# Decay attention into a mixture of experts on one core: the reciprocals of the row sums are spread by ScalarE, and the order of all steps is laid out anew

## The chip, the core and the metric

The kernel runs on one core of a Trainium2 chip. Its engines work side by side, each through its own instructions in order: TensorE (PE: matmuls; its weight loads are PEld), VectorE (DVE), ScalarE (ACT), GpSimd (POOL) and SyncE (SP), which here issues the DMA transfers. Engines wait for each other on semaphores. The metric is the device time of one execution in microseconds (us). For the kernel before it is 650.12 us, the median of three runs (650.10, 650.12, 650.39).

## What is computed

```python
# decay attention, B=8, H=8, S=576, D=64
scores = (q @ k.T) / sqrt(D) + cum[i] - cum[j]      # cum = cumsum(log f); causal
attn   = exp(scores - rowmax) / (rowsum + 1e-9)
x      = (attn @ v)                                  # laid out as [B, S, 512]
# mixture of E=4 experts, the best K=2 for each row
w      = softmax over the two best logits of x @ w_gate
for e in range(E):                                   # each expert is a causal attention on x
    y_e  = softmax(causal((x @ wq[e]) @ (x @ wk[e]).T / sqrt(64))) @ (x @ wv[e]) @ wo[e]
    out += (e is chosen) * w_e * y_e
```

## The kernel before

**Units.** The work is cut into 48 units of two heads or two experts: `a{b}_{p}` is head pair p (0 to 3) of batch b, `m{b}_{p}` expert pair p (0 or 1). Each unit goes through the same generators, and a name ends in its unit (`ka_a1_1` is tile ka of unit a1_1):

- `prep_attn` makes the operands of the scores. All products are made in two parts, a rounded value and its rest; the rests of a head pair are two subtractions at L406 (64x1152 each, on VectorE for nearly all pairs), into `ka`, which the scores read. For the experts `moe_front` (gates at L504 to L532) and `prep_moe` (matmuls `pp` at L551) do this.
- `max_pass` finds a maximum for each row: matmuls into `m` (L625), masked maxima on VectorE at L631, L647, L680 and L687 into `mxs`, a transposition of `mxs` on TensorE (`mp`, L692), and from there ScalarE (`ms`, L695) and a DMA into the operand `kq`.
- `scores` makes the products s0 to s3 (L726 reads `ka`, L727 reads `kq`), ScalarE takes the exponentials into `P` and `pl` (L744 to L784), GpSimd cuts them at the diagonal (L713, L747, L786) and adds them to the row sums `R` (L792 to L798).
- `attend` multiplies by the values (L817) and ScalarE brings the result to `ot` (L841, L843).
- `row_sums` does two units at once, so there are 24 of them: 16 of heads, 8 of experts. Matmuls with a column of ones make `sm`; VectorE transposes it into `zt` (L870), adds 1e-9 (L873), takes the reciprocal `rc` of 18 columns (L875; experts: times the gate, L878), spreads each of these 18 numbers over 32 equal columns of `zt` (L881, 128x576, called the fill below), and transposes that into `rr` (L884). A DMA spreads `rr` to `bt`, with which `apply_rows` multiplies `ot` (L902). The tile of a row_sums is named by the first unit of the two: `zt_a0_2` holds the sums of a0_2 and a0_3.
- `project_out` multiplies by wo (`po`, L952), and the result leaves by DMA.

**Order.** Each generator stops at every `yield`. A table of two-digit numbers, ORDER, says which generator goes on next; another one, SLOTS, says which of a tile's buffers each use takes. At the end each engine's instructions are tied to the order in which they were written, so nothing overtakes on an engine. The two tables lay down the whole order of the kernel.

The loop that plays ORDER, and the tie:

```python
for x, y in zip(digits[::2], digits[1::2]):
    i = DIGITS.index(x) * len(DIGITS) + DIGITS.index(y)
    if i not in started:
        started[i] = iter(tasks[i]())
    next(started[i], None)
```

Of the kernel before, what the change touches and what calls it, by code (L numbers as in the profile page):

```python
# [32 lines left out]
040j0c0h0h0h0h0h0c0e0e0e0e0e030e08080e0e0e0e0e0e080808080808080e0808080e030e0o0e0h08080e080e04030j0j0j080e080808
080808080808080j0j0j0j0j0j0j08080o0t030o0o0f0f0j0j0j0j0j0j0j0j0j0j0j0j0j0j0o080A090j030f0j0h090v0o0t0j0q0f080f0f
0f0f0f0f0f0f090f0f0o080f0f0f0q0q0q0j0f0q0f0f0f0q0q0q0j0q0q0q0f0f0f0p0f0t0t0t0f4w4w4w080q0q0q0q0q0q0q030q0q0q0q0q
0q0q0i0A080f080q0f0t0k0k0k0k0k0k0k0k0k0k0k0k0k0f0k0o0a0q0q0q0k0k0k0k0a0k0k0k0k0k0k0a0a0v0v0v0v0a0a0v0v0v0v0v0k0F
0v0g0k0a0v0v0v0v0v0A0A0A0F0g0g0f0f0k0k0f0v0v0v0v0v0u0C0k0v0a0t0f0l0q0C0C0v0C0C0r0r4A0v0v0l040C0t0C0C0k0k0k0C0C0r
# [1022 lines left out]
```

## Time and profile before

| | us |
|---|---|
| median of three runs | 650.12 |
| the profiled execution | 650.38 |
| its span in the trace | 648.6 |
| TensorE busy | 629.9 (97%) |
| VectorE busy | 571.6 (88%) |
| GpSimd busy | 479.0 (74%) |
| ScalarE busy | 470.1 (72%) |
| mean granted TensorE clock | 0.996 of full speed |

The profile is of one execution. Its span runs from the first to the last instruction; 1.8 us of the execution lie around it. A row of a timeline gives the start of an instruction, its duration, the engine, the line, what it writes and reads, and in square brackets how long the engine stood idle ahead of it and who released it. Instructions overlap a little at their ends, so a start minus the start before is often the better price.

### The profile page before, as it was taken

What the parts mean: (1) busy time and instruction counts of PE and PEld (TensorE: products, weight loads), DVE (VectorE), ACT (ScalarE), POOL (GpSimd) and SP (SyncE); (2) the same over time, 40 slices, a digit from 0 to 9 for tenths busy, and PEclk for the clock granted to TensorE, in tenths of its full rate; (3) what the DMA queues carried; (4) which work ended last, traced back from release to release, by engine and by line L of the source; (5) the groups of instructions that cost most, each with busy time, mean ns of one, the idle gap of its engine ahead of it and who ended that gap; (6) DMA issues with size and microseconds to landing.
All of it is one profiled execution on the core that took longest, in us unless ns stands there. A gap on an engine that the chain in (4) does not pass through costs nothing.

```text
span 648.6 us, 15367 instructions
## 1 busy us (share of the span) xinstructions
PE 629.9 (97%) x5303; PEld 539.0 (83%) x5303; DVE 571.6 (88%) x1565; ACT 470.1 (72%) x1033; POOL 479.0 (74%) x759
## 2 busy tenths in 40 slices
PE   8898998999999999999999999999999999999997
PEld 6675898887978889889797898878988788979976
DVE  6899998999999989988989989999898999986762
ACT  7896785786769757797497875788768886556634
POOL 9999695878888776669578966967778758833850
PEclk9999998999999999999999999999999999999999
DMA  6556324443534454550643531753524632523125
GB/s 211 159 161 171 98 74 113 132 120 116 126 95 116 126 162 111 127 133 22 169 108 83 163 102 57 187 145 114 150 75 113 190 72 44 146 60 72 54 70 199
DMA packets 33532, 76.91 MB, mean 119 GB/s; under 512 B 4395, under 2 KB 4875, under 8 KB 33455
## 3 DMA queue, kind: packets, MB, share of 16 engines
q1 hardware_dynamic: 33455, 75.94, 43.4%
q8 instruction: 42, 0.69, 0.4%
q14 instruction: 35, 0.29, 0.1%
HBM read 32.86 MB, written 10.35 MB: 67 GB/s over the span
## 4 chain that ended last, share of the span: by engine, by line
PE 85%; DVE 9%; issue 2%; POOL 2%; ACT 1%; DMA 0%; SPq 0%; POOLq 0%; DVEq 0%; ACTq 0%
PE pp_m L551 15%; PE ob_a L817 9%; PE po L952 7%; PE pv L446 7%; PE s_a L726 7%; PE m_a L625 7%; PE s_a L727 6%; PE ob_m L817 4%; PE m_m L625 4%; PE s_m L726 4%; PE s_m L727 4%; DVE ka_a L406 3%; PE oa_a L817 3%; PE sm_a L855 2%; PE oa_m L817 2%
## 5 line engine op out<-in xcount | busy, mean ns | idle before, releaser
L726 PE MATMUL s_a<-ka_a 128*128 128x320 f32 (+4 forms) x384 | 105.0, 299 | 3.3 <-DVE mx_m L680 1.7
L727 PE MATMUL s_a<-kq 128*128 128x320 f32 (+4 forms) x384 | 103.6, 297 | 1.2 <-DMA kq<-ms_a 1.1
L631 DVE CUSTOM_DVE_ANT_0 junk_a<-m_a,mask 128x192 bf16<-128x192 f32 (+2 forms) x186 | 86.5, 484 | 7.7 <-PE m_a L625 4.1
L625 PE MATMUL m_a<-kq 128*128 128x448 f32 (+2 forms) x372 | 77.5, 302 | 1.7 <-DVE mxs_a L631 1.2
L713 POOL TENSOR_SCALAR_AFFINE_SELECT P_a<-P_a 128x128 f32<-128x128 f32 x128 | 53.1, 425 | 34.0 <-ACT P_a L762 17.6
L726 PEld LDWEIGHTS s_a<-ka_a 128*128 128x128 f32 (+1 forms) x384 | 70.1, 183 | 6.1 <-issue 4.1
L559 ACT ACTIVATE kq<-pp_m 64x288 fp32r<-64x288 f32 x128 | 51.8, 405 | 31.7 <-PE pp_m L551 29.8
L792 POOL TENSOR_TENSOR R_a<-P_a 128x448 f32<-128x448 f32 x64 | 73.5, 1149 | 0.0
L727 PEld LDWEIGHTS s_a<-kq 128*128 128x128 f32 (+1 forms) x384 | 69.6, 183 | 2.6 <-DMA kq<-ms_a 1.6
L564 DVE TENSOR_TENSOR ka_m<-pp_m,kq 64x288 fp32r<-64x288 f32 x128 | 58.3, 455 | 12.9 <-ACT kq L559 10.6
L817 PE MATMUL ob_a<-P_a,va 128*64 128x320 f32 (+1 forms) x512 | 67.6, 406 | 0.0
L794 POOL TENSOR_TENSOR R_a<-R_a,P_a 128x320 f32<-128x320 f32 x64 | 64.7, 1012 | 3.3
L747 POOL TENSOR_SCALAR_AFFINE_SELECT P_a<-P_a 128x256 f32<-128x256 f32 x64 | 34.5, 545 | 42.7 <-ACT P_a L744 41.8
L625 PEld LDWEIGHTS m_a<-kq 128*128 128x128 f32 x372 | 57.3, 180 | 6.4 <-DVE mxs_a L631 2.2
L817 PEld LDWEIGHTS ob_a<-P_a,va 128*64 128x64 f32 x512 | 35.6, 137 | 24.2
L406 DVE TENSOR_TENSOR ka_a<-xin_a,ka_a 64x1152 fp32r<-64x1152 f32 x32 | 53.2, 1663 | 0.8
L726 PE MATMUL s_m<-ka_m 128*128 128x192 f32 (+2 forms) x192 | 51.9, 297 | 0.0
L744 ACT ACTIVATE P_a<-s_a 128x512 f32<-128x512 f32 x64 | 36.7, 596 | 20.8 <-PE s_a L727 20.2
L727 PE MATMUL s_m<-kq 128*128 128x192 f32 (+2 forms) x192 | 51.1, 294 | 0.0
L406 DVE TENSOR_TENSOR ka_a<-xin_a,kq 64x1152 fp32r<-64x1152 f32 x29 | 49.6, 1709 | 0.9
L631 DVE CUSTOM_DVE_ANT_0 junk_m<-m_m,mask 128x192 bf16<-128x192 f32 (+2 forms) x96 | 45.0, 484 | 5.3 <-PE m_m L625 4.5
L796 POOL TENSOR_TENSOR R_a<-R_a,P_a 128x192 f32<-128x192 f32 x64 | 45.8, 717 | 2.8
(206 smaller groups left out, 2095.2 us busy)
## 6 DMA issues: line engine op xcount, KB each, us to landing
xin_a<-in_qk_dram SPq DMA_DIRECT2D x32, 576.0 KB
va<-in_v_dram SPq DMA_DIRECT2D x32, 320.0 KB
bt_a<-rr_a SPq DMA_DIRECT2D x32, 288.0 KB
ka_m<-kq SPq DMA_DIRECT2D x32, 288.0 KB
kq<-ka_a SPq DMA_DIRECT2D x30, 288.0 KB
...
```

The costliest lines, as they stand in the source:

```text
L406: eng.tensor_tensor(lo, x[at], hi.bitcast(F32), ALU.subtract)
L551: nc.tensor.matmul(pp[:, :HS], w[:, c, es], x[c][:, gs], start=(n == 0), stop=(n == 3 * KC - 1))
L559: nc.scalar.activation(hv[h], src[h], AF.Copy)
L564: nc.vector.tensor_tensor(lo[:, h, gs], src[h], hv[h].bitcast(F32), ALU.subtract)
L625: nc.tensor.matmul(dst, qB[0:K, h, i0 : i0 + dst.shape[0]], kB[0:K, h, j0:j1], start=True, stop=True)
L631: nc.vector.tensor_tensor_reduce(jk[:, :n], src, mask[:, MW - n :], 1.0, init, ALU.add, ALU.max, acc)
L713: return nc.gpsimd.affine_select(pv, pv, [[1, 128]], ALU.is_ge, 0.0, base=0, channel_multiplier=-1)
L726: nc.tensor.matmul(dst, kaf[:, c : c + m], qA[:, h, i0:i1], start=True, stop=False)
L727: nc.tensor.matmul(dst, kqf[0:K, c + h * S : c + h * S + m], qB[0:K, h, i0:i1], start=False, stop=True)
L792: g.tensor_tensor(r[:, h, 128:S], q[:, 320:768], q[:, 768:1216], ALU.add)
L794: g.tensor_tensor(r[:, h, 256:S], r[:, h, 256:S], q[:, 1216:1536], ALU.add)
L817: mm = nc.tensor.matmul(dst[64 * h : 64 * h + 64, c0 : c0 + rhs.shape[-1]], vs[h][0:kp, blk], rhs, start=first, stop=last,)
```

## The change

The fill at L881 is an activation of ScalarE with the function Copy, where it was a copy by VectorE. ORDER and SLOTS are new from the first line to the last. The instructions are otherwise the same ones: 24 fills (16 of heads, 8 of experts) go from VectorE to ScalarE, no other instruction is added, dropped or given to another engine.

```diff
@@ ORDER and SLOTS (every line differs; two stand for all) @@
-P 01201201201201201202010210121021201201201210210120
+P 01201201201201201201201210212012012012012012012012
...
@@ row_sums @@
             nc.vector.tensor_tensor(rc, rc, moe[b]["gc"], ALU.mult)
             yield
 
-        nc.vector.tensor_copy(zt, rc.unsqueeze(2).to_broadcast([128, 18, 32]))
+        nc.scalar.activation(zt, rc.unsqueeze(2).to_broadcast([128, 18, 32]), AF.Copy)
         yield
         rr = strip("rr" + nm)
         nc.vector.transpose(rr, zt.rearrange("p c k -> p (c k)"))

What moves is shown at three places. A row of the lists below is one instruction: its line, operation, output<-inputs (the tile's name with a running number) and shape; `mxs` rows without an input read out the accumulator of the row above.

VectorE, ahead of the transposition `mp_a1_1` on TensorE, which needs all of `mxs_a1_1`. Before:

```order
L680 TENSOR_TENSOR mx0_a1_1_943<-m3_a1_1_933,mask_83 64x128
L406 TENSOR_TENSOR ka_a1_1_759<-xin_a1_1_624,ka_a1_1_759 64x1152
L687 TENSOR_REDUCE mxs_a1_1_687<-mx0_a1_1_943 64x2
L631 ISA junk_a1_2_970,mxs_a1_2_940<-m0_a1_2_966,mask_83 128x192
L631 ISA mxs_a1_2_940 128x1
L647 TENSOR_REDUCE mxt_a1_2_972<-m0_a1_2_966 128x1
L631 ISA junk_a1_1_985,mxs_a1_1_687<-m3_a1_1_983,mask_83 128x320
```

After:

```order
L680 TENSOR_TENSOR mx0_a1_1_948<-m3_a1_1_942,mask_83 64x128
L687 TENSOR_REDUCE mxs_a1_1_672<-mx0_a1_1_948 64x2
L631 ISA junk_a1_1_975,mxs_a1_1_672<-m3_a1_1_951,mask_83 128x320
L631 ISA mxs_a1_1_672 128x1
L631 ISA junk_a1_2_982,mxs_a1_2_973<-m0_a1_2_979,mask_83 128x192
L631 ISA mxs_a1_2_973 128x1
L647 TENSOR_REDUCE mxt_a1_2_984<-m0_a1_2_979 128x1
```

The last maximum of a1_1 now stands ahead of the first two of a1_2, and the subtraction into `ka_a1_1`, which stood between, has gone to an earlier place (ahead of the transposition into `rr_a0_0`).

VectorE at the row sums of a0_2 and a0_3. Before:

```order
L873 TENSOR_SCALAR rc_a0_2_1123<-zt_a0_2_1120 128x18
L875 RECIPROCAL rc_a0_2_1123<-rc_a0_2_1123 128x18
L881 COPY zt_a0_2_1120<-rc_a0_2_1123 128x576
L884 STREAM_TRANSPOSE rr_a0_2_1134<-zt_a0_2_1120 128x576
L406 TENSOR_TENSOR ka_a1_2_916<-xin_a1_2_661,kq2_96 64x1152
```

After:

```order
L873 TENSOR_SCALAR rc_a0_2_1112<-zt_a0_2_1108 128x18
L875 RECIPROCAL rc_a0_2_1112<-rc_a0_2_1112 128x18
L884 STREAM_TRANSPOSE rr_a0_2_1116<-zt_a0_2_1108 128x576
L406 TENSOR_TENSOR ka_a1_2_874<-xin_a1_2_582,kq2_96 64x1152
L902 TENSOR_TENSOR ot_a0_1_677<-bt_a0_0_1_926,ot_a0_1_677 128x576
```

The transposition into `rr` follows the reciprocal directly. ScalarE at the same place, before:

```order
L779 ACTIVATE P_a1_0_1002<-s3_a1_0_1070 128x320
L784 ACTIVATE pl1_92<-s3_a1_0_1070 64x128
L744 ACTIVATE P_a1_1_1099<-s0_a1_1_1090 128x512
L744 ACTIVATE P_a1_1_1099<-s0_a1_1_1104 128x512
L756 ACTIVATE P_a1_1_1099<-s1_a1_1_1127 128x2x256
```

After:

```order
L779 ACTIVATE P_a1_0_1007<-s3_a1_0_1076 128x320
L695 ACTIVATE ms_a1_2_1105<-mp_a1_2_1100 10x128
L784 ACTIVATE pl1_92<-s3_a1_0_1076 64x128
L881 ACTIVATE zt_a0_2_1108<-rc_a0_2_1112 128x576
L936 ACTIVATE lx0_1119<-xh_a0_0_0_1035 128x64
L936 ACTIVATE lx0_1119<-xl_a0_0_0_1083 128x64
L744 ACTIVATE P_a1_1_1123<-s0_a1_1_1056 128x512
```

The fill stands between the last exponential of a1_0 and the first of a1_1. Such a pair, reciprocal and transposition with nothing between them on VectorE, also stands at a2_0, m6_0 and m7_0; at the other 20 row sums other work of VectorE stands between.

VectorE between the maxima of a2_2 and those of a2_3. Before:

```order
L406 TENSOR_TENSOR ka_a2_3_2237<-xin_a2_3_2086,kq1_95 64x1152
L406 TENSOR_TENSOR ka_a2_3_2237<-xin_a2_3_2086,ka_a2_3_2237 64x1152
L687 TENSOR_REDUCE mxs_a2_2_1945<-mx0_a2_2_2253 64x2
L631 ISA junk_a2_2_2318,mxs_a2_2_1945<-m3_a2_2_2316,mask_83 128x320
L631 ISA mxs_a2_2_1945 128x1
L870 STREAM_TRANSPOSE zt_m0_0_2347<-sm0_m0_0_2320 128x288
L870 STREAM_TRANSPOSE zt_m0_0_2347<-sm1_m0_0_2321 128x288
L528 COPY gc0_2350<-pg0_2330 128x16
L532 COPY gc0_2350<-pg0_2330 128x2
L873 TENSOR_SCALAR rc_m0_0_2371<-zt_m0_0_2347 128x18
L406 TENSOR_TENSOR ka_a2_2_2020<-xin_a2_2_1905,kq0_94 64x1152
L406 TENSOR_TENSOR ka_a2_2_2020<-xin_a2_2_1905,ka_a2_2_2020 64x1152
```

After:

```order
L406 TENSOR_TENSOR ka_a2_2_2030<-xin_a2_2_1883,kq0_94 64x1152
L631 ISA junk_a2_2_2246,mxs_a2_2_1956<-m3_a2_2_2235,mask_83 128x320
L631 ISA mxs_a2_2_1956 128x1
L510 RECIPROCAL sm0_2129<-sm0_2129 128x5
L929 TENSOR_TENSOR xl_a1_2_1_2249<-ot_a1_3_1982,xh_a1_2_1_2243 128x576
L512 TENSOR_TENSOR gt0_2065<-gt0_2065,sm0_2129 128x20
L406 TENSOR_TENSOR ka_a2_2_2030<-xin_a2_2_1883,ka_a2_2_2030 64x1152
L528 COPY gc0_2341<-pg0_2313 128x16
L870 STREAM_TRANSPOSE zt_m0_0_2343<-sm0_m0_0_2303 128x288
L532 COPY gc0_2341<-pg0_2313 128x2
L870 STREAM_TRANSPOSE zt_m0_0_2343<-sm1_m0_0_2304 128x288
L873 TENSOR_SCALAR rc_m0_0_2349<-zt_m0_0_2343 128x18
```

The pair of subtractions of a2_2 now stands where that of a2_3 stood, ahead of the transpositions into `zt_m0_0`; the pair of a2_3 follows behind `rc_m0_0`.

## Rows read from the trace of the kernel before

**Rows 1.** The page's first part: busy us of each engine, share, instructions.

```profile
PE 629.9 (97%) x5303; PEld 539.0 (83%) x5303; DVE 571.6 (88%) x1565; ACT 470.1 (72%) x1033; POOL 479.0 (74%) x759
```

**Rows 2.** Busy time by stretch: each engine's us, granted clock, DMA share, GB/s.

```profile
12.00:98.00 86.00, 76.54 (x614) 61.94 (x611) 79.45 (x216) 69.93 (x136) 78.77 (x117) 1.00 0.49 137
98.00:105.00 7.00, 5.27 (x31) 4.68 (x23) 6.77 (x14) 3.40 (x6) 2.50 (x5) 0.76 0.23 50
105.00:165.00 60.00, 58.47 (x524) 51.17 (x523) 55.87 (x153) 45.71 (x106) 47.79 (x76) 1.00 0.48 129
165.00:612.00 447.00, 446.01 (x3816) 386.56 (x3815) 404.55 (x1132) 325.67 (x737) 326.19 (x524) 1.00 0.43 112
612.00:648.50 36.50, 32.71 (x253) 25.61 (x251) 17.02 (x46) 17.38 (x43) 12.96 (x20) 0.98 0.40 127
```

**Rows 3.** TensorE's timeline: the three starts after long waits for VectorE.

```profile
64.98 0.27 PE L692 MATMUL mp_a<-ident,mxs_a 128*10 128x128 f32 x1 [1.31 <-DVE mxs_a L631]
...
100.41 0.33 PE L726 MATMUL s_a<-ka_a 128*128 128x192 f32 x1 [1.73 <-DVE mx_m L680]
...
157.98 0.33 PE L726 MATMUL s_a<-ka_a 128*128 128x192 f32 x1 [1.53 <-DVE ka_a L406]
```

**Rows 4.** The fills by line L881: ns min/median/max, first and last start.

```profile
L881 DVE COPY zt_a<-rc_a x16: 446/460/1056, 56.7 to 571.0; 128x576 f32<-128x576 f32 x16
L881 DVE COPY zt_m<-rc_m x8: 459/468/1640, 162.1 to 628.5; 128x576 f32<-128x576 f32 x8
```

**Rows 5.** ScalarE's copies at L921, by form: busy us, mean ns, idle before.

```profile
L921 ACT ACTIVATE xh_a<-ot_a 128x576 fp32r<-128x576 f32 x32 | 21.8, 682 | 9.4 <-DVE ot_a L902 9.1
```

**Rows 6.** Timeline of VectorE and ScalarE at 630 us: from one to the other and back.

```profile
630.41 0.75 DVE L902 TENSOR_TENSOR ot_m<-bt_m,ot_m 128x576 f32<-128x576 f32 x1
...
631.26 0.63 ACT L921 ACTIVATE yh_m<-ot_m 128x512 fp32r<-128x512 f32 x1 [5.46 <-DVE ot_m L902]
...
631.92 0.69 DVE L929 TENSOR_TENSOR yl_m<-ot_m,yh_m 128x512 fp32r<-128x512 f32 x1 [0.76 <-ACT yh_m L921]
```

**Rows 7.** VectorE's timeline ahead of 64.98: the last maxima.

```profile
63.75 0.36 DVE L631 CUSTOM_DVE_ANT_0 junk_a<-m_a,mask 128x192 bf16<-128x192 f32 x1
...
64.03 0.48 DVE L647 TENSOR_REDUCE mxt_a<-m_a 128x1 f32<-128x320 f32 x1
64.44 0.48 DVE L631 CUSTOM_DVE_ANT_0 junk_a<-m_a,mask 128x320 bf16<-128x320 f32 x1
```

**Rows 8.** VectorE's and ScalarE's timeline at 71 us, the row sums of a0_2.

```profile
71.88 0.27 DVE L875 RECIPROCAL rc_a<-rc_a 128x18 f32<-128x18 f32 x1
72.18 0.46 DVE L881 COPY zt_a<-rc_a 128x576 f32<-128x576 f32 x1
72.67 0.78 DVE L884 STREAM_TRANSPOSE rr_a<-zt_a 128x576 f32<-128x576 f32 x1
...
71.03 0.27 ACT L784 ACTIVATE pl<-s_a 64x128 f32<-64x128 f32 x1
71.19 1.07 ACT L744 ACTIVATE P_a<-s_a 128x512 f32<-128x512 f32 x2
```

**Rows 9.** VectorE's timeline ahead of 157.98: the subtractions of a2_3, then of a2_2.

```profile
147.28 2.89 DVE L406 TENSOR_TENSOR ka_a<-xin_a,kq 64x1152 fp32r<-64x1152 f32 x1
150.19 1.46 DVE L406 TENSOR_TENSOR ka_a<-xin_a,ka_a 64x1152 fp32r<-64x1152 f32 x1
...
153.63 2.26 DVE L406 TENSOR_TENSOR ka_a<-xin_a,kq 64x1152 fp32r<-64x1152 f32 x1
155.90 1.94 DVE L406 TENSOR_TENSOR ka_a<-xin_a,ka_a 64x1152 fp32r<-64x1152 f32 x1
```

**Rows 10.** VectorE's and GpSimd's timeline ahead of 100.41.

```profile
96.02 3.51 DVE L406 TENSOR_TENSOR ka_a<-xin_a,ka_a 64x1152 fp32r<-64x1152 f32 x1
...
95.69 1.27 POOL L354 TENSOR_TENSOR ql<-st_q,qh 128x512 fp32r<-128x512 f32 x1
...
97.19 1.14 POOL L792 TENSOR_TENSOR R_a<-P_a 128x448 f32<-128x448 f32 x1
```

More of the change, by code (lines that the diff above doesn't have):

```diff
@@ L33 @@
[L33 to L37, printed above, removed]
@@ new lines @@
+4y4y004x4x4y024y4y4A4y4y4y4y004w4A4w4A4A4w4w4w4A4A4A014A4A4A4A054w4w4w4w4w4w4w050505054w4w4w4w4w4w024w4w4w4w4w4w
+4w4w4w4w4w4w4w4w4w0000000000024w024w0202020202020202020c4z4w4w4w4w4w4z074w07074w0207020202020202020202024A4w4w4w
+4w05020202020202050c060c4w4w4w4w07074w4w4A4w020202054w4w0c0c034y0c4y030307070c4w4w4w070703034A4A0703030303070707
+030707030303030303074y0h0e4z0707070303030303030303030303034z0707070707074z0e0e0e070e4z0707074z4z0e0e0e0e0e040c0e
+0e0e0e0e0e0e0e0j0e0h0h0h0c0h0e0e08080h0e0e03080e0808080h08080808080808080808080o08080t0A0e030j0j0j0j0j0j0j080808
@@ new lines @@
+03084w4w0e0e040e0j0j0j0808080o0808030j0j0j0j0j0j0j0j0j0j084w080j0j0j0j0j090e0v0e0o090j0q0t0h0j0o0f0o0f0o0o0j0j0f
+0f0f0f0f0f0f030f0f0f0f0f0f0f0f0f0q0q0q0q0q0q0k0q080f0f0q0q0q0f0d080f0f0k0f0f0i080t0f0t030q080k0k0k0k0k0q0q0q0q0q
+0q0t0q0q040q0A0f0q0k0k0k0k0k0k0k0q0q0f0q0q0a0k0k0t094A0f0a0a0q0q0k0k0k0k0k0k0a0a0k0k0k0k0k0A0F0v0v0v0v0v0v0v0A0A
+0f0f0q0q0v0v0v0a0g0t0k0a0f0F0a0a0k0g0v0v0v0v0v0v0v0v0v0v0v0v0v0f0k0l0t0k0C0v0v0l0C0C0C0C0C0C0C0v0o0k0C0v0C0C0r0r
+0r0r0r0r0r0r0r0r0r0v0k0C0b0v0f0k0r0r0b0C0C0C0C0C0r0r0r0r0r0r0w0r0p0C0C0C0C0C0C0C0C0r0r0b0F0F0w0m0C0C0g0r0r0r0C0r
@@ new lines @@
+0m0F0m0m0m0m0m0r0b0b0A0w0r0w0w0w0w0w0w0w0l0N0b0H0s0b0H0O0H0H0b0H0r0H0H0w0H0w0s0w0s0H0w0w0m0n0n0b0b0w4A0m0M4y4y4A
+0N4y0w0n0n0H0w0w0w0n0n0w0n0w0R0R0n0w0w0R0H0M0M0n0R0N0C0N0w0w0H0H0H0H0H0C0H0H0H0H0H0H0H0H0H0w0w0A0N0u0A0N0N0N0N0N
+0R0r0w0M0R0M0r0N0N0N0N0N0N0N0N0N0w0w0w0w0N0N0N0N0N0N0N0N0N0N0N0N0N0N0N0N0D0D0D4A0D0D0D0O0O0D0D0O0O0O0D0D0D0D0Y0D
+0D0D0N0r0B0O0O0H0O0O0O0M0M0D0D0D0D0M0D0D0D0D0D0D0H0H0H0H0O0O0r0r0O0O0O0O0O0M0N0w0Y0O0N0O0O0Y0D0R0D0x0y0+0O0F0F0O
+0F4A0x0M0D0O0O0y0M0M0Y0y4A0I0y0x0I0I0I0I0I0I0I0I0I0I0I0I0I0Y0I0I0I0I0I0I0I0I0I110I0I0I0O0O0O0O0O0y0I0Y0D0+0I0R0R
@@ new lines @@
+0R0+0+0Z0R0+0R0R0R0R0R0R0I0D0S0I0R0R0R0R0R0R0y0y0I0I0I0+0+0+0+0+0R0n0R0R0R0R0y0R0R0R0R0R0R0R0R0P0P0S0P0P0P0P0P0S
+0S0b0S0n0S0S0S0M0P0P0G0P0P0S0P0P0S0S0P0P0P0P0D0D0+0z0M0M0I0P0S0S0S0S0D110S0P0P0P0S0S0S0S0D0S0y0S0P110P0R0R0P0P0P
+0P0M0M0M0+0S0S0S0M0S0+0M0+0+0z0+0M0+0M0M0P0P0M0z0+0+0+0S0S0+0M0M0M0M0+0+110+0K0K0K0K0K0+110M180E0E0M0J0S0P0P0M0M
+0S0M0M0+0z0+0K1d0Y0Y0K0K0K180E110T0T0+111a0M0z0T0T0T0T0T0M0T0T0T0T0T0J0J190T0T0z0+0T0T0T0T0M0P131313131313131313
+130P0T0P130T0T0T180Q0Q0T0-0-0L0L0M130-0z0M0T0T0T0+180T0T130z131313131313130T1k180Q0M0-0-0-13130-0-0-130-0-0-0-0-
@@ new lines @@
+1313130M0M0z0-0L0-0T0T0-0-0-0T0T0-0-1a1a1a1a1a1a0-1a0-0-0-131313130-0-111a1a0U140U1f1a0U1d1d0L0L0L1d1d0L1a1a1a1a
+1a1a1a1a1a1a1a1a1a0M1814140L141a0M0L0M0T0M181k1k1414141414141414141414141a0-0-0-1l100V0M1a1a1l1l0M0V0M1B0V0V144A
+18141f140-0-1a14141414101414141d1l1l1l1l1p1m1k1f1f1f1f1f1f1k1l1l1l1l1l1l1l1l1l1p1p1p1f1a1l1f1b1f1l0V1d0-1b1b1414
+1b1b1d0V1l1b1e1b1b0-1b1b1l1b141f1l1f101k1f1l141f1f1f1f1l0V1l1l1f1f1f1f1f1f1f1f1l1l1l1l1l1l1l1l1l1l1k1l1k1k0V1b1b
+1b1b1b1b1b1b1b1b1b4y1f1b1b1b1b1b1b1b1f1f1f0V4A1p1l1p1p1m1m1m1m1m1m1m1m1m14141m121q1p1p1p1p1p1p1p1p1p1p1p1p1p4A14
@@ L123 @@
+4n4n4n4n4n474n4n4n4n4n4n4n4q4q4q4q4n4n4n484n4n4n4n48484h484q4q4q4p4p4p4p4k4k4k4k4k4k4k4k4k4k4k4k4k3L4k4k4k4n4n4n
+4n4n4n4k4k4k4q4q4r4r4r4r4r4r4r4r4r4r4r4r4r4r4r4r4h4n4h4k4k4h48484k4h4h4h4h4h4r4r4r4r4r4r4r4h4r4r4r4k4r4r4r4r4r4r
+4r4r3L3L3L3L3L3L3L4k4k4k3L4k4k4k4k4k4k4g4k4k4g4g4k4k4k4o4k4t4i4k4o4o4t4t4t4t4k4k4t4t4t4t4s4s4i4i4t4i4i4i4i4i4i4u
+4u4u4u4s4u4u4u3L3L3L3L3L3L3L3L3L4j4j4j4j4i4j4j4u4u4u4j4j4j4j4j4j4j4j4j4i4v4u4v4v4v4v4v4v4v4j4v4v4v4v4v4v4v4v4v4v
 4v4v4v
```

168 lines of the change are left out of this document (72 added, 96 removed).

## The prediction

> **What bounds the kernel now.** I read the page's engine totals first: TensorE is busy 97% of the span, VectorE 88%, ScalarE 72% [rows 1]. An average says little of an edit that lies in one place, so the second view is busy time by stretch [rows 2]. It divides the kernel in two. From 165 to 612 us TensorE works 446.0 of 447.0 us: nothing that VectorE is spared there can come out at the end, except by keeping TensorE full. From 12 to 98 us TensorE works 76.5 of 86 and VectorE 79.5, and around 100 us VectorE works 6.8 of 7: there VectorE is the one that is waited for. The third view, TensorE's timeline, gives the places [rows 3]: starts after 1.31 us at 64.98, 1.73 at 100.41 and 1.53 at 157.98, each released by VectorE. Only these, with the clock behind the second, can pay for anything: in 98 to 105 us the granted clock is 0.76 on average. At the lower level, 1.2 GHz, for x us of these 7, 1 - 0.5x/7 = 0.76 gives x = 3.4; work of 1.7 us at 2.4 GHz took 3.4, so 1.7 us were lost there. Behind the waits at 64.98 and 157.98 the stretches show 1.00 [rows 2].
>
> All sums are made against the profiled execution, 650.38 us (span 648.6, and 1.8 around it); the median of the three runs is 0.26 lower, 650.12, and the forecast is put there.
>
> **The fills.** VectorE loses 24 fills of 0.46 us [rows 4]; by these medians 11.0 us of 571.6. ScalarE's price for 128x576 out of SBUF into SBUF is not shown for a broadcast input; the nearest row is its copy of 128x576 at L921, 0.68 us [rows 5], and I take that: 24 x 0.68 = 16.4 us on an engine with 470.1 busy. Going over and back costs little: VectorE's L902 ends at 630.41 + 0.75 = 631.16 and ScalarE starts at 631.26, and ScalarE's 631.26 + 0.63 = 631.89 lets VectorE start at 631.92, so 0.10 + 0.03 us [rows 6]. The chain from reciprocal to transposition thus takes 0.81 in place of about 0.49 (72.18 to 72.67 [rows 8]): 0.32 longer. For 20 of the fills VectorE has other work between reciprocal and transposition, so that it does not stand and gains the whole 0.46. For a0_2, a2_0, m6_0 and m7_0 the two follow directly, and VectorE stands.
> Of these four only a0_2 lies where VectorE bounds: **+0.3**. Its bounds: -0.46 if VectorE's spare time takes the stand, and +2 if ScalarE comes late to the fill; it comes behind work like the 1.07 us pair at L744 or the 0.27 us at L784 [rows 8], and before, L784 was done at 71.30, 0.85 us ahead of the reciprocal's end at 72.15, so I take it as free. The 18 fills behind 165 us and ahead of 612, and their stands, count 0, covered by TensorE's full queue (446.0 of 447.0); with that cover gone the stands would cost 0.3 each. In the last 36 us TensorE works 32.7 [rows 2], and its output products fill it while m7_0's sums are spread: between 0 and +0.4 for this last fill, taken at 0.
> Here the Trainium skill speaks: "Perfetto Trace Analysis", section "Optimizing Scalar/DVE Operations", says that VectorE is faster on a copy where a fast mode applies, but that giving work to ScalarE may pay where VectorE is saturated. By its first half, applied to all 24, the edit would cost some 24 x 0.2 = 5 us, by its second it pays; the stretch rows say that the second holds up to 165 us and neither behind it.
>
> **The moves, place by place.**
> At 64.98 TensorE waits 1.31 for the last maximum of a1_1. Ahead of that stood two steps of a1_2, 63.75 to 64.03 and 64.03 to 64.44, 0.69 us in all [rows 7]; they now stand behind it. The fill of a0_0, 0.46, is gone as well from the work ahead. VectorE thus arrives 1.15 earlier. But TensorE has fewer products ahead of the place too, since the products of a1_2 have moved with their maxima: I count half of VectorE's gain, **-0.6**; bounds 0 (TensorE arrives as much earlier) and -1.3 (the whole wait).
> At 157.98 TensorE waits 1.53 for the second subtraction of a2_2, which ends at 155.90 + 1.94 = 157.84. In the new order the pair of a2_2 stands where that of a2_3 stood, which had ended at 150.19 + 1.46 = 151.65 [rows 9], some 6 us ahead of the need. The pair of a2_3 comes behind it, and the scores of a2_3 are wanted about a unit's time later (an estimate: 648.6 us by 48 units, 13.5 us). So this wait goes, **-1.5**; the next to be late is the first maximum of a2_3, behind one subtraction of 1.4 to 2.9 us, which keeps the bounds at 0 and -1.5.
> At 100.41 TensorE waits 1.73 behind a subtraction of 3.51 us at 96.02, which runs beside GpSimd's two-input additions of 1.27 and 1.14 us [rows 10]; such a subtraction alone takes 1.46 (150.19 [rows 9]), so 2.05 us of it is the meeting of the two. The new order has other neighbours there, but the same two engines with the same kinds of work and the same consumer, so whether they meet is not laid down: **0**, bounds -3.4 (the wait and the clock's 1.7 both go) and +1.7 (a further dip of the clock, as at this one place, behind some other wait).
> The sum: +0.3 - 0.6 - 1.5 + 0 = **-1.8**, 650.38 - 1.8 = 648.58, on the median's footing **648.3 us**. By another road: ahead of 165 us VectorE is spared five fills, four of heads and m0_0's at 162.1 us [rows 4], 5 x 0.46 = 2.3, less 0.3 for the stand with its 0.46 not gained, 0.8, makes -1.5. The two agree near enough.
>
> **The rivals.**
> A. *The stretch up to 165 us is not paced by VectorE's work but by what feeds it* (TensorE's own products, ScalarE's exponentials: 69.9 of 86 us, GpSimd 78.8 of 86 [rows 2]). GpSimd is as full as VectorE from 12 to 98 us and its work is unchanged. Then the waits of rows 3 turn up at other names: a gain of 0 to 0.8, time about 650.0. For it: GpSimd's 78.8; against: all three waits were released by VectorE.
> B. *ScalarE's queue is tied to VectorE's.* The fill at a0_2 waits for the reciprocal with the exponentials of a1_1 behind it. With L784 done 0.85 us early, ScalarE stands 0.85 and then works 0.68, so the exponentials leave 1.5 us later than if the fill were not there. TensorE's next products wait for the banks that these exponentials free, and GpSimd, the fullest, for their results. It decides if ScalarE has under 1.5 us in hand at a0_2; it works 69.9 of 86, so in the mean it has some slack but less than elsewhere. Then the moves' gain of 2.1 stays, but 1.5 is lost at a0_2, 1.5 more at one of a0_0, a1_0 or a1_2 and 1.7 by a dip of the clock like that at 100 us: +2.6, 652.7 us. **This one ends slower than before.**
> C. *The meetings of VectorE and GpSimd fall otherwise.* If the subtraction ahead of 100.41 takes 1.5 rather than 3.5, that wait and the dip go, -3.4 more: 645 us; with half of it, 646.6.
> The Trainium skill has a rule for this, "SBUF — State Buffer", section "Who interferes with whom": VectorE instructions with two inputs in SBUF share a port pair with GpSimd, and the one that issues second blocks. The 3.51 beside 1.46 agrees with it; by this rule the fills' move alone would change no subtraction's price, only the new order does.
> D. *The edit does not do what it says*: the instructions are the same but for the 24 fills, so this reduces to the order being worth nothing, as A.
>
> **How the numbers follow.** The forecast case, waits at 64.98 and 157.98 eased and the rest as before: 0.44. A: 0.24, of which most lies within 0.2%. C: 0.14. B: 0.18. A measurement of this kernel can tell about 0.2%, 1.3 us, from no change. Faster by more than that, below 648.8: C, and nine tenths of the forecast case less its weaker end, 0.14 + 0.38 = 0.52. Within: A, the forecast's weak end and a little of B: 0.28. Slower, above 651.4: 0.20, B and the far side of A. The range: the low end takes in half of C, 645.5; the high end reaches past 650.0 of A to the near part of B, 651.6. Below and above lie about 0.08 and 0.14.
>
> **What would show it.** In the profile of the changed kernel: L881 on ScalarE, 24 of about 0.68 us (over 0.9: the price is wrong). VectorE idle about 0.8 us ahead of the transposition into `rr_a0_2`, a2_0, m6_0 and m7_0; much more at the first means that ScalarE came late, B. TensorE's wait ahead of `s0_a2_2` gone, or else the -1.5 is wrong; that ahead of `mp_a1_1` near 0.7. If waits of the same length stand at other names and stretch 12 to 98 still has 76 of 86, A. If the granted clock stays at 1.00 around 100 us, C; a second dip elsewhere is B's sign. From 165 to 612 us TensorE should stay at about 1 us short of full: if it falls further, the stands behind 165 us are not covered and the prediction is wrong in its largest zero.

## The result

The changed kernel takes 657.06 us (median of five runs, 656.45 to 658.59) where the kernel before takes 650.12: a ratio of 1.0117 (95% interval 1.0104 to 1.013; the two medians alone give 1.0107), 7 us slower. The forecast was 648.3. The profiled execution took 657.54 us, with a span of 655.5, 6.9 more than before.

First the page's engine totals of the changed kernel, in the form of [rows 1], and the busy time by stretch, in the form of [rows 2]:

```profile
PE 633.0 (97%) x5303; PEld 542.0 (83%) x5303; DVE 564.6 (86%) x1541; ACT 480.9 (73%) x1057; POOL 469.9 (72%) x759
```

```profile
12.00:98.00 86.00, 72.72 (x546) 59.11 (x544) 75.73 (x197) 64.20 (x121) 71.37 (x106) 0.96 0.46 133
98.00:105.00 7.00, 6.90 (x58) 5.79 (x58) 6.43 (x21) 6.16 (x12) 4.18 (x10) 1.00 0.08 17
105.00:165.00 60.00, 59.39 (x537) 51.16 (x534) 55.59 (x151) 46.45 (x103) 51.11 (x78) 1.00 0.47 127
165.00:612.00 447.00, 443.33 (x3758) 385.30 (x3757) 396.05 (x1102) 333.72 (x758) 314.78 (x514) 1.00 0.43 112
612.00:655.50 43.50, 39.82 (x341) 32.00 (x340) 22.91 (x65) 22.37 (x57) 17.60 (x32) 1.00 0.40 116
```

VectorE has become lighter, as planned (564.6 in place of 571.6 us). The loss lies ahead of 98 us, where TensorE works 72.7 us in place of 76.5 and the clock has fallen to 0.96 on average, and, smaller, from 165 to 612 us, where TensorE lacks 3.7 us of a full stretch and lacked 1.0. In between things went better than before: around 100 us the dip of the clock is gone.

TensorE's timeline shows the places (start, duration, and in brackets the idle time ahead and who ended it), to be held against [rows 3]:

```profile
64.55 1.32 PE L625 MATMUL m_a<-kq 128*128 128x192 f32 x4 [4.49 <-DVE mxs_a L631]
67.09 0.38 PE L692 MATMUL mp_a<-ident,mxs_a 128*10 128x128 f32 x1 [1.22 <-DVE mxs_a L631]
...
95.23 0.33 PE L726 MATMUL s_a<-ka_a 128*128 128x192 f32 x1 [1.19 <-DVE ka_a L406]
```

Two waits of 4.49 and 1.22 us stand where one of 1.31 stood. What VectorE did meanwhile is in its own timeline:

```profile
55.22 0.47 DVE L631 CUSTOM_DVE_ANT_0 junk_a<-m_a,mask,mxt_a 128x256 bf16<-128x256 f32 x1
...
55.74 7.57 DVE L406 TENSOR_TENSOR ka_a<-xin_a,ka_a 64x1152 fp32r<-64x1152 f32 x1
63.33 0.78 DVE L884 STREAM_TRANSPOSE rr_a<-zt_a 128x576 f32<-128x576 f32 x1
...
66.53 0.49 DVE L631 CUSTOM_DVE_ANT_0 junk_a<-m_a,mask 128x320 bf16<-128x320 f32 x1
```

One subtraction, the second one into `ka_a1_1`, took 7.57 us. The same work takes 1.46 us in [rows 9]. It is the step that stands ahead of `rr_a0_0` in the new order. GpSimd's timeline beside it:

```profile
55.48 0.58 POOL L796 TENSOR_TENSOR R_a<-R_a,P_a 128x192 f32<-128x192 f32 x1
56.03 2.23 POOL L792 TENSOR_TENSOR R_a<-P_a 128x448 f32<-128x448 f32 x2
58.23 1.68 POOL L794 TENSOR_TENSOR R_a<-R_a,P_a 128x320 f32<-128x320 f32 x2
59.88 1.12 POOL L796 TENSOR_TENSOR R_a<-R_a,P_a 128x192 f32<-128x192 f32 x2
60.97 1.11 POOL L792 TENSOR_TENSOR R_a<-P_a 128x448 f32<-128x448 f32 x1
62.03 0.09 POOL L621 MEMSET mxs_a<- 64x2 f32 x1
62.16 1.86 POOL L794 TENSOR_TENSOR R_a<-R_a,P_a 128x320 f32<-128x320 f32 x1
```

From 55.48 to 62.08 GpSimd adds without a pause. The subtraction, issued 0.26 us after the first of these additions, ends 63.3 - 62.1 = 1.2 us after the last: nearly all of its own work comes behind the row (the first subtraction into `ka_a1_1`, at 51.04 in this run, took 1.35 us alone). The next addition, L794, then takes 1.86 us where its like takes 0.84 (two in 1.68): now GpSimd stood for VectorE. The clock's dip begins behind the first wait (stretches of busy time, same columns as above):

```profile
63.40:67.00 3.60, 1.30 (x4) 0.73 (x4) 3.53 (x14) 0.00 (x0) 0.62 (x1) 0.75 0.44 83
67.00:70.00 3.00, 2.91 (x13) 2.91 (x14) 2.46 (x11) 1.23 (x3) 0.41 (x1) 0.50 0.33 103
70.00:73.00 3.00, 3.00 (x15) 2.79 (x14) 1.55 (x6) 2.35 (x5) 2.04 (x5) 0.66 0.36 110
```

At 0.50 for 3 us and at 0.66 for 3 us TensorE lost 1.5 + 1.0 = 2.5 us. The 0.75 of the first row is 1.8 us at the lower level; TensorE mostly waited there.

The fills themselves came out as priced. By line, and at a0_2 (ScalarE's row, then VectorE's):

```profile
L881 ACT ACTIVATE zt_a<-rc_a 128x576 f32<-128x576 f32 x16 | 10.9, 681 | 7.7 <-DVE rc_a L875 7.6
...
78.04 0.68 ACT L881 ACTIVATE zt_a<-rc_a 128x576 f32<-128x576 f32 x1 [1.84 <-DVE rc_a L875]
...
78.75 0.78 DVE L884 STREAM_TRANSPOSE rr_a<-zt_a 128x576 f32<-128x576 f32 x1 [0.75 <-ACT zt_a L881]
```

A fill takes 0.68 us, and VectorE stood 0.75 us for the one at a0_2. ScalarE stood 1.84 us there, more than the 0.85 that I had counted.

### The profile page after: what moved, and what is told of

It reads as the page before. It is cut to its first block, busy times and chain, and to the rows that moved or that the text cites. A ratio compares the mean times of both kernels' runs of the same rounds, so it can differ in the third digit from the quotient of the medians.

```text
span 655.5 us, 15384 instructions
## 1 busy us (share of the span) xinstructions
PE 633.0 (97%) x5303; PEld 542.0 (83%) x5303; DVE 564.6 (86%) x1541; ACT 480.9 (73%) x1057; POOL 469.9 (72%) x759
## 4 chain that ended last, share of the span: by engine, by line
PE 76%; DVE 10%; ACT 4%; POOL 4%; DMA 3%; issue 2%; SPq 0%; POOLq 0%; DVEq 0%; ACTq 0%
PE pp_m L551 14%; PE ob_a L817 7%; PE s_a L726 6%; PE po L952 6%; PE s_a L727 6%; PE pv L446 6%; PE m_a L625 6%; PE ob_m L817 4%; PE m_m L625 4%; PE s_m L727 3%; PE s_m L726 3%; DVE ka_a L406 3%; PE oa_a L817 3%; PE sm_a L855 2%; DVE junk_a L631 2%
## 5 line engine op out<-in xcount | busy, mean ns | idle before, releaser
L726 PE MATMUL s_a<-ka_a 128*128 128x320 f32 (+4 forms) x384 | 105.7, 301 | 2.4 <-DVE ka_a L406 1.2
L631 DVE CUSTOM_DVE_ANT_0 junk_a<-m_a,mask 128x192 bf16<-128x192 f32 (+2 forms) x186 | 86.6, 484 | 7.7 <-PE m_a L625 5.2
L625 PE MATMUL m_a<-kq 128*128 128x448 f32 (+3 forms) x372 | 78.1, 305 | 7.2 <-DVE mxs_a L631 6.2
L792 POOL TENSOR_TENSOR R_a<-P_a 128x448 f32<-128x448 f32 x64 | 74.6, 1166 | 0.0
L726 PEld LDWEIGHTS s_a<-ka_a 128*128 128x128 f32 (+1 forms) x384 | 70.3, 183 | 4.9 <-ACT kq L559 1.4
L713 POOL TENSOR_SCALAR_AFFINE_SELECT P_a<-P_a 128x128 f32<-128x128 f32 x128 | 51.2, 408 | 29.5 <-ACT P_a L779 14.2
L747 POOL TENSOR_SCALAR_AFFINE_SELECT P_a<-P_a 128x256 f32<-128x256 f32 x64 | 37.8, 599 | 47.9 <-ACT P_a L744 47.3
L625 PEld LDWEIGHTS m_a<-kq 128*128 128x128 f32 x372 | 58.5, 182 | 12.8 <-DVE mxs_a L631 7.9
L817 PE MATMUL ob_a<-P_a,va 128*64 128x320 f32 (+1 forms) x512 | 67.6, 406 | 0.0
L794 POOL TENSOR_TENSOR R_a<-R_a,P_a 128x320 f32<-128x320 f32 x64 | 63.8, 997 | 3.3
L406 DVE TENSOR_TENSOR ka_a<-xin_a,ka_a 64x1152 fp32r<-64x1152 f32 x32 | 58.3, 1821 | 0.8
L817 PEld LDWEIGHTS ob_a<-P_a,va 128*64 128x64 f32 x512 | 36.0, 137 | 23.8
L726 PE MATMUL s_m<-ka_m 128*128 128x256 f32 (+3 forms) x192 | 51.4, 294 | 0.0
L727 PE MATMUL s_m<-kq 128*128 128x256 f32 (+3 forms) x192 | 50.8, 293 | 0.0
L631 DVE CUSTOM_DVE_ANT_0 junk_m<-m_m,mask 128x448 bf16<-128x448 f32 (+2 forms) x96 | 44.6, 486 | 6.4 <-PE m_m L625 5.5
L744 ACT ACTIVATE P_a<-s_a 128x512 f32<-128x512 f32 x64 | 36.6, 593 | 13.1 <-PE s_a L727 12.4
L796 POOL TENSOR_TENSOR R_a<-R_a,P_a 128x192 f32<-128x192 f32 x64 | 43.1, 674 | 2.8
L406 DVE TENSOR_TENSOR ka_a<-xin_a,kq 64x1152 fp32r<-64x1152 f32 x29 | 41.5, 1431 | 2.7 <-PE s_m L726 1.9
```

Source lines behind the costliest of these rows:

```text
L406: eng.tensor_tensor(lo, x[at], hi.bitcast(F32), ALU.subtract)
L625: nc.tensor.matmul(dst, qB[0:K, h, i0 : i0 + dst.shape[0]], kB[0:K, h, j0:j1], start=True, stop=True)
L631: nc.vector.tensor_tensor_reduce(jk[:, :n], src, mask[:, MW - n :], 1.0, init, ALU.add, ALU.max, acc)
L713: return nc.gpsimd.affine_select(pv, pv, [[1, 128]], ALU.is_ge, 0.0, base=0, channel_multiplier=-1)
L726: nc.tensor.matmul(dst, kaf[:, c : c + m], qA[:, h, i0:i1], start=True, stop=False)
L727: nc.tensor.matmul(dst, kqf[0:K, c + h * S : c + h * S + m], qB[0:K, h, i0:i1], start=False, stop=True)
```

## The experiments

The theories: **P**, the subtraction into `ka_a1_1` stands beside GpSimd's additions, and that is the loss; **F**, the fills on ScalarE are the loss; **S**, VectorE and GpSimd share a rate, so that any meeting stretches both. All medians are set against the kernel before on the same chip (650.02, 649.94 and 650.22 us in the three sets of runs that follow). Diffs of the order show the rows that move on the engine named; where a line stands twice, once with - and once with +, it is one instruction.

**The subtraction back behind L680** (VectorE, changed kernel):

```diff
+L884 STREAM_TRANSPOSE rr_a0_0
+... four maxima of a1_1, L680 mx0_a1_1 ...
 L406 TENSOR_TENSOR ka_a1_1
-L884 STREAM_TRANSPOSE rr_a0_0
-... four maxima of a1_1, L680 mx0_a1_1 ...
```

> The changed kernel with one step put back: the second subtraction into ka_a1_1 (L406) stands behind mx0_a1_1 (L680), as in the kernel before, no longer ahead of rr_a0_0. Theory P (that subtraction starts at 55.74 us, just inside an unbroken row of GpSimd additions, and stands still until GpSimd's first pause at 62.03): VectorE now does the transposition and the maxima first and reaches the subtraction at about 58.7; it still waits for the pause and ends near 63.3, so about 4.6 us in place of 7.57, but only one maximum comes behind it: TensorE's mp_a1_1 at about 64.3 in place of 67.1, a time of about 654, or 652 if the clock's dip behind it goes as well. Rival F (the fills on ScalarE cost the time): 657, no change.

Measured: 654.32 us (ratio 1.0069, 1.0052 to 1.0086). VectorE's timeline:

```profile
55.63 0.78 DVE L884 STREAM_TRANSPOSE rr_a<-zt_a 128x576 f32<-128x576 f32 x1
...
58.55 4.77 DVE L406 TENSOR_TENSOR ka_a<-xin_a,ka_a 64x1152 fp32r<-64x1152 f32 x1
```

4.77 us in place of 4.6, and 2.7 us won of the 7, as P has it. F falls as the whole cause. The transposition, at 55.63 in the midst of the additions, takes its usual 0.78: this kind of instruction does not stand.

**An earlier memset as a pause** (GpSimd, changed kernel):

```diff
 L792 TENSOR_TENSOR R_a0_2
+L621 MEMSET mxs_a1_2
 L792 TENSOR_TENSOR R_a0_3
 L794 TENSOR_TENSOR R_a0_2
 L794 TENSOR_TENSOR R_a0_3
 L796 TENSOR_TENSOR R_a0_2
 L796 TENSOR_TENSOR R_a0_3
 L792 TENSOR_TENSOR R_a0_3
-L621 MEMSET mxs_a1_2
 L794 TENSOR_TENSOR R_a0_3
```

> The changed kernel with one GpSimd step moved: the memset of mxs_a1_2 (0.09 us), which made the first pause in the row of additions, stands five additions earlier, behind the second addition L792 of a0_2. Nothing moves on VectorE. Theory P (a subtraction with two inputs in SBUF stands until GpSimd pauses): it starts near 55.7 as before, gets going at the pause at about 57.1 and ends near 58.4, about 2.7 us in place of 7.57; TensorE's waits of 4.49 and 1.22 shrink to about 2 in all; time 651 to 653.5. Rival S (the two engines share a rate, so the subtraction goes on slowly beside all additions): still about 7 us, 657. Rival F (fills): 657.

Measured: 657.17 us (1.0114, 1.0099 to 1.0129): no change, the expectation of P missed. (The memset stands six additions earlier; the expectation says five.) VectorE's row and three of GpSimd's:

```profile
55.73 7.60 DVE L406 TENSOR_TENSOR ka_a<-xin_a,ka_a 64x1152 fp32r<-64x1152 f32 x1
...
57.09 0.09 POOL L621 MEMSET mxs_a<- 64x2 f32 x1
...
60.99 1.12 POOL L792 TENSOR_TENSOR R_a<-P_a 128x448 f32<-128x448 f32 x1
62.19 1.86 POOL L794 TENSOR_TENSOR R_a<-R_a,P_a 128x320 f32<-128x320 f32 x1
```

The memset is not what lets VectorE go. With the memset away, GpSimd still pauses from 60.99 + 1.12 = 62.11 to 62.19, ahead of the addition that takes the result of the one just before it, and there the subtraction got going. S would fit this run as well. So P was narrowed to **D**: VectorE gets its turn where an addition of GpSimd has to wait for the one right before it. In the new order, as in the old one, the additions of a0_2 and a0_3 alternate, so that hardly any depends on its neighbour.

**The changed order with the fills on VectorE, and the order before with the fills on ScalarE:**

```diff
-        nc.scalar.activation(zt, rc.unsqueeze(2).to_broadcast([128, 18, 32]), AF.Copy)
+        nc.vector.tensor_copy(zt, rc.unsqueeze(2).to_broadcast([128, 18, 32]))
```

> The changed kernel's order with the fills (L881) on VectorE as before, 0.46 us each. Rival F (ScalarE's fills cost the time): near 650. Theory P: the subtraction of 7.6 us stays, since the row of additions stays; the five fills ahead of 165 us add up to 2 us: 657 to 659.

> The order of the kernel before with the fills on ScalarE: the edit of the one line alone. Theory P: the order makes the loss, not the fill, so 649 to 651.5. Rival F: 654 or more.

Measured: 667.56 us (1.0277, 1.0261 to 1.0294) and 657.61 us (1.0125, 1.0102 to 1.0147). The first misses both expectations: with the fills back on VectorE the new order is slower still, so F is not what makes its loss. The second misses P's and meets F's, 654 or more: in the old order the fills on ScalarE do lose, and "the order makes the loss, not the fill" is wrong there. The new order alone costs 17.5 us, the fills alone 7.6, both together 7.0, so the two halves cannot be judged one by one. VectorE's timeline of the first shows one reason:

```profile
55.60 6.78 DVE L881 COPY zt_a<-rc_a 128x576 f32<-128x576 f32 x1
62.41 1.90 DVE L406 TENSOR_TENSOR ka_a<-xin_a,ka_a 64x1152 fp32r<-64x1152 f32 x1
```

The fill, back on VectorE right ahead of the subtraction, is now the one that stands, 6.78 us until 62.38, so a plain copy of f32 stands as well. The second (ScalarE's row, then TensorE's) shows the rival B of the prediction at work, in the old order:

```profile
518.13 0.68 ACT L881 ACTIVATE zt_a<-rc_a 128x576 f32<-128x576 f32 x1 [2.94 <-DVE rc_a L875]
...
521.73 0.41 PE L625 MATMUL m_a<-kq 128*128 128x320 f32 x1 [2.63 <-ACT outb L956]
```

A fill put where VectorE's fill stood makes ScalarE stand 2.94 us for the reciprocal; the copy at L956 behind it is late, and TensorE waits 2.63 us for that. From 165 to 612 us TensorE lacks 4.6 us of a full stretch in this run, where it lacked 1.0; the rest of the 7.6 us I have not traced.

**One addition behind the one it depends on** (GpSimd, changed kernel):

```diff
 L792 TENSOR_TENSOR R_a0_2
+L794 TENSOR_TENSOR R_a0_2
 L792 TENSOR_TENSOR R_a0_3
-L794 TENSOR_TENSOR R_a0_2
 L794 TENSOR_TENSOR R_a0_3
```

> The changed kernel with one GpSimd addition moved: L794 of a0_2, second head, stands right behind the addition L792 whose result it takes, no longer behind the first addition of a0_3. The same additions; VectorE's order untouched. The memset, moved ahead, did not let the subtraction go; in all three runs with the place it got going where an addition follows the one it depends on (a pause of 0.07 to 0.1 us, as at 62.1). Theory D (VectorE gets the port at a pause that such a dependence makes): the subtraction starts near 55.73, gets going at 57.1, ends near 58.4: 2.7 us in place of 7.57; TensorE's mp_a1_1 some 4.5 to 5 us earlier, the dip of the clock shorter or gone; 650 to 653. Rival S (a shared rate, given by the number of additions beside it): no change, 657.

Measured: 650.48 us (1.0013, 1.0003 to 1.0022): 6.6 us of the 7 are back, by the place of one 0.9 us addition. VectorE's row and two of GpSimd's:

```profile
55.74 2.65 DVE L406 TENSOR_TENSOR ka_a<-xin_a,ka_a 64x1152 fp32r<-64x1152 f32 x1
...
56.03 1.14 POOL L792 TENSOR_TENSOR R_a<-P_a 128x448 f32<-128x448 f32 x1
57.25 1.87 POOL L794 TENSOR_TENSOR R_a<-R_a,P_a 128x320 f32<-128x320 f32 x1
```

The pause is 57.17 to 57.25, the subtraction ends 1.2 us after it (58.39), and the L794 behind it takes 1.87. The same additions, another order, another price: S falls, and this run goes as D has it. The clock's mean from 12 to 98 us is 1.00 again.

**The same at a second place** (GpSimd, the run before this one as base):

```diff
 L792 TENSOR_TENSOR R_a1_0
+L794 TENSOR_TENSOR R_a1_0
 L796 TENSOR_TENSOR R_a1_1
 L792 TENSOR_TENSOR R_a1_1
 L794 TENSOR_TENSOR R_a1_1
 L796 TENSOR_TENSOR R_a1_1
 ... three selects ...
-L794 TENSOR_TENSOR R_a1_0
```

> As the run with the one addition moved, and the same done at a second place: L794 of a1_0, second head, right behind its L792, ahead of two independent additions at 92 us, where the subtraction into ka_a1_3 took 4.17 us. Theory D: that subtraction gets going at 92.2 in place of 93.9 and ends 1.6 us earlier, TensorE's wait of 1.19 ahead of s0_a1_3 goes: 1.0 to 1.5 us below the run with one move. Rival S: no difference to it.

Measured: 648.66 us (0.9989, 0.9979 to 0.9998), 1.8 below the run with one move, a little more than expected. By the order of VectorE's instructions this subtraction goes into `ka_a1_2`, and TensorE's wait of 1.19 us is ahead of s0_a1_2; the expectation names a1_3. It is shown here with one move and with two:

```profile
83.82 4.17 DVE L406 TENSOR_TENSOR ka_a<-xin_a,ka_a 64x1152 fp32r<-64x1152 f32 x1
```

```profile
83.80 2.51 DVE L406 TENSOR_TENSOR ka_a<-xin_a,ka_a 64x1152 fp32r<-64x1152 f32 x1
```

**The kernel before with the subtraction early** (VectorE):

```diff
+L406 TENSOR_TENSOR ka_a1_1
 L884 STREAM_TRANSPOSE rr_a0_0
 ... four maxima of a1_1, L680 mx0_a1_1 ...
-L406 TENSOR_TENSOR ka_a1_1
 L687 TENSOR_REDUCE mxs_a1_1
```

> The kernel before, fills on VectorE, with one step moved: the second subtraction into ka_a1_1 ahead of rr_a0_0, where the changed kernel has it. Theory D: it starts at 58.2, in the row of GpSimd additions that goes from 57.3 to 62.3 with a memset but without a dependent pair, so it ends near 63.5: 5.3 us in place of 2.49; the last maximum of a1_1 and TensorE's mp_a1_1 come about 2.8 us later: 653 to 655 with a dip of the clock, 652 without. If the memset at 59.19 let it go: 2.3 us and 650. Rival F (the new fills make the loss): 650.

Measured: 656.64 us (1.0102, 1.0087 to 1.0117). One step moved in the old kernel, fills on VectorE, gives nearly the whole loss; VectorE's row and two of GpSimd's:

```profile
58.19 5.22 DVE L406 TENSOR_TENSOR ka_a<-xin_a,ka_a 64x1152 fp32r<-64x1152 f32 x1
...
59.09 0.10 POOL L621 MEMSET mxs_a<- 64x2 f32 x1
...
62.27 1.86 POOL L794 TENSOR_TENSOR R_a<-R_a,P_a 128x320 f32<-128x320 f32 x1
```

The duration is as expected (5.3), past a memset again; the time is 1.6 us above the upper end, since two stretches show a dip of the clock in this run (0.96 from 12 to 98 us and 0.97 from 105 to 165), where I had allowed for one.

**The two moves with the fills back on VectorE** (the one line, as above):

> The run with two additions moved, with the fills back on VectorE: what the change of engine alone is worth in this order. By the prediction's term, up to 165 us five fills of 0.46 less 0.3 to 0.8: 1.5 us, so 650. Theory D: a copy on VectorE can itself stand beside GpSimd's additions, and in this order it stands right ahead of the two subtractions that meet them: the fill of a0_0 at 55.6 waits for the pause at 57.1 (2 us), the subtraction behind it for the next one at 60.2 (to 61.5, 3 us later than with the fill on ScalarE): 653 to 660.

Measured: 661.68 us (1.0172, 1.0137 to 1.0208), 13 us above the same order with the fills on ScalarE (by the medians of two sets). Two rows of VectorE's timeline and two of GpSimd's:

```profile
55.59 1.86 DVE L881 COPY zt_a<-rc_a 128x576 f32<-128x576 f32 x1
57.49 1.92 DVE L406 TENSOR_TENSOR ka_a<-xin_a,ka_a 64x1152 fp32r<-64x1152 f32 x1
...
57.22 0.97 POOL L794 TENSOR_TENSOR R_a<-R_a,P_a 128x320 f32<-128x320 f32 x1
58.13 2.27 POOL L792 TENSOR_TENSOR R_a<-P_a 128x448 f32<-128x448 f32 x1
```

At the first place it costs 1 us, not the 3 expected, and D falls short: the subtraction did not wait for the next pause. It got going when the addition under way ended (57.22 + 0.97 = 58.19), and the next addition, which depends on nothing just before it and has no pause ahead of it, took 2.27 us where such a one takes 1.1. What sets this meeting apart is that the addition under way had itself begun behind a pause.

So read, the thirteen traces agree. At boundaries between two additions where a subtraction of L406 or a fill of VectorE stood waiting (its turn taken to be 1.2 us or 0.4 us ahead of its end), it got its turn at each of the 108 with a pause. At those without one it was passed over 58 times and got its turn nine times. In all nine the addition under way had begun behind a pause; of the 58 one had, and there VectorE came 0.03 us before the boundary. Many of these meetings recur from run to run, and the pattern was read off afterwards; no run was made to test it.

TensorE's stretches, first two with the fills on VectorE, then from 165 us on with the same order and the fills on ScalarE:

```profile
12.00:98.00 86.00, 75.96 (x573) 63.22 (x572) 76.63 (x213) 66.16 (x126) 72.87 (x113) 0.96 0.47 133
165.00:612.00 447.00, 438.65 (x3690) 378.18 (x3689) 400.52 (x1094) 319.41 (x723) 308.81 (x503) 1.00 0.42 111
...
165.00:612.00 447.00, 443.60 (x3798) 385.04 (x3797) 393.48 (x1096) 331.57 (x755) 317.35 (x518) 1.00 0.43 113
```

Behind 165 us TensorE lacks 8.4 us of a full stretch, with the fills on ScalarE 3.4; ahead of 98 us the clock is at 0.96 on average, in place of 1.00. So both parts lose, and in an order laid for fills on ScalarE the engine of the fill is worth far more than the 1.5 us of the prediction.

**Late steps, the subtraction last, and all of it.** Three runs on top of the two moves. The first moves two small steps of VectorE behind 165 us:

```diff
-L508 TENSOR_SCALAR sm1            (ahead of L680 mx0_a3_1)
+L508 TENSOR_SCALAR sm1            (behind the last maximum of a3_1 and the first of a3_2)
-L878 TENSOR_TENSOR rc_m3_0        (ahead of the first maxima of a5_3)
+L878 TENSOR_TENSOR rc_m3_0        (behind the first two)
```

> The run with two additions moved, and two small VectorE steps moved behind 165 us: the addition L508 on 128x5 (1.67 us beside a row of GpSimd additions at 208 us, 0.2 alone) from ahead of the last maxima of a3_1 to behind them, and the product L878 of m3_0 (1.24 us beside an addition at 381 us) behind the first two maxima of a5_3. TensorE waits 1.17 at 210 and 0.69 at 383 us behind these. Theory D (behind 165 us too, what stands beside GpSimd's additions is given on to TensorE): 1.2 to 1.8 us below the run with two moves, 646.8 to 647.5. The zero of the prediction (behind 165 us TensorE's full queue hides it): no difference, 648.7.

The second puts the subtraction into `ka_a1_1` behind the last maximum of a1_1, the third does all:

```diff
-L406 TENSOR_TENSOR ka_a1_1
 L884 STREAM_TRANSPOSE rr_a0_0
 ... all that is left of a1_1's maxima ...
+L406 TENSOR_TENSOR ka_a1_1
```

> The run with two additions moved, and the second subtraction into ka_a1_1 behind the last maximum of a1_1, so that nothing of it stands ahead of TensorE's mp_a1_1; the scores of a1_1 come later. Theory D: the subtraction starts near 59.4, gets going at the pause at 60.2 and ends at 61.5, in time; the wait of 1.42 ahead of mp_a1_1 goes: 1.0 to 1.5 us below the run with two moves, 647.2 to 647.7.

> All of these moves in one: two additions of GpSimd, the two late steps of VectorE, and the subtraction into ka_a1_1 behind the last maximum. If the gains add up: 2.5 to 3 us below the run with two moves, 645.5 to 646.3, and below the kernel before by 0.6%.

Measured: 648.24 us (0.9964, 0.9946 to 0.9982), 646.91 us (0.9949, 0.9932 to 0.9966) and 645.71 us (0.9927, 0.99 to 0.9955). The small step at L508, in the changed kernel and with the late moves:

```profile
216.64 1.67 DVE L508 TENSOR_SCALAR sm<-sm 128x5 f32<-128x5 f32 x1
```

```profile
209.36 0.17 DVE L508 TENSOR_SCALAR sm<-sm 128x5 f32<-128x5 f32 x1
```

The late moves alone gave 0.4 us by the medians of two different sets of runs, short of the 1.2 expected and not to be told from nothing; in the trace TensorE works 444.48 us from 165 to 612, 0.9 more than with the two moves alone. On top of the third move, in one set, they gave 646.91 - 645.71 = 1.2. The subtraction behind the last maximum gave 1.75 (by the medians of two sets), more than expected. It did not wait for the pause that the expectation names: it started at 59.31, within the addition at 59.16 that had begun behind a pause, and took 1.93 us, while the next two additions, L796, took 2.25 us in place of 1.13. With all moves the kernel takes 645.7 us, as expected, 0.7% less than the kernel before.

## Why the prediction was wrong

*What bounds the kernel.* Right up to 165 us: there the longest waits are for VectorE, before and after. But the three places were not all. In the kernel before TensorE also waits 1.66 us at 55.22, longer than at 64.98 and 157.98, for a transposition of VectorE behind a subtraction of 4.38 us, the first into `ka_a1_1`, which stands beside GpSimd; in the new order this subtraction takes 1.35 us and the wait is gone:

```profile
50.39 4.38 DVE L406 TENSOR_TENSOR ka_a<-xin_a,kq 64x1152 fp32r<-64x1152 f32 x1
...
55.22 0.87 PE L817 MATMUL oa_a<-P_a,va 128*64 128x256 f32 x8 [1.66 <-DVE zt_a L870]
```

The statement that from 165 us on nothing that VectorE is spared can come out at the end is half the truth: what VectorE is made late by does come out. TensorE lacks 3.7 us of that stretch in the changed kernel, 1.0 before, 8.4 with the two moves and the fills on VectorE. The largest zero of the sum was +2.7, though not by the fills' stands, which the prediction gave as its sign. The waits found there are 1.01 us at 219.40, 0.54 at 392.44 and 1.11 at 452.57, all for VectorE's maxima. Ahead of the first two VectorE stands beside GpSimd with a small step, L508 (1.67 us) and L878 (1.24 us); the third I have not traced. The first:

```profile
219.40 0.27 PE L692 MATMUL mp_a<-ident,mxs_a 128*10 128x128 f32 x1 [1.01 <-DVE mxs_a L631]
```

*The wait at 64.98, -0.6.* This is the step that failed. The list of the new order shows the subtraction into `ka_a1_1` gone to an earlier place; the prediction counted the two maxima and the fill that no longer stand ahead, and gave the moved subtraction the price that it had had, as if a price were the instruction's own. It had weighed such a meeting with GpSimd only at 100.41, where the trace of before shows it [rows 10] (it shows one at 50.39 as well), and bounded its loss at 1.7. What GpSimd does beside the new place was not looked up. Measured: 4.49 + 1.22 - 1.31 = +4.4 us, and 2.5 for the clock. That this one subtraction makes most of the loss is shown twice: undone by an addition's place (-6.6 of 7), and made in the old kernel by that one move (+6.7).

*The fill, +0.3 at a0_2.* Price (0.68) and stand (0.75 of VectorE) were right. ScalarE's stand of 1.84 is rival B's beginning; in the changed kernel no long wait of TensorE follows from it, but in the old order with the new fills it does (2.63 us at 521.73). B had a chance of 0.18 and a price of 652.7; the time came out beyond that, through another mechanism. What the term left out is that a fill on VectorE is a copy that can itself stand beside GpSimd (6.78 us at 55.60): in this order the change of engine alone is worth 13 us (661.68 to 648.66), not 1.5.

*The wait at 157.98, -1.5.* Right: it is gone, and TensorE works 59.4 of the 60 us from 105 to 165, where it worked 58.5.

*The place at 100.41, 0 with -3.4 as the lower end.* Most of the lower end came. The subtraction into `ka_a1_3` takes 2.51 us in place of 3.51, the product behind it, s0_a1_3, starts at 107.50 after a wait of 0.61, for ScalarE, in place of 1.73, and the clock stays at 1.00: -1.1 - 1.7 = -2.8. A smaller meeting turned up ahead of it (4.17 us for the subtraction into `ka_a1_2`, which took 1.44 before; waits of 1.19, 0.29 and 0.24 us), +1.7.

These sizes add up to +4.4 + 2.5 - 1.5 - 2.8 + 1.7 + 2.7 = +7.0, where the spans differ by 6.9. That it comes so near is in part chance, since the list is not whole: it leaves out the wait of 1.66 us that is gone, and shorter ones that came, 0.85 at 37.95 and 0.60 at 82.53. By the totals TensorE is busy 3.1 us longer (633.0 - 629.9) and idle 3.8 us longer (22.5 in place of 18.7). Rival C's mechanism was the right one, but I had given it a gain only: the meetings did fall otherwise, one better and one far worse. With the two worst meetings taken out the kernel takes 648.66, near the forecast of 648.3, which is partly luck: it is the sum of larger gains and of a loss behind 165 us that had been put at zero.

The Trainium skill, "SBUF — State Buffer", section "Who interferes with whom", says that a VectorE instruction with two inputs in SBUF, or a copy or scalar operation in its two-port mode, contends with GpSimd, and that the one that issues second blocks fully while the other's instruction lasts. The trace agrees that it blocks, for the subtraction (7.57 beside 1.46), the copy (6.78 beside 0.46) and the scalar operation at L508 (1.67 beside 0.17); whether the last two ran in that mode no run shows. It differs in how long: the subtraction stood not for one instruction but through eight additions. The prediction quoted the part on two inputs and drew from it only that the fills would change no subtraction's price; the rule asks for every moved step what the other engine does at its new place.
